# Weight decoding given to VectorE from the third retention chunk on instead of the second

## The chip, the cores and the metric

The program runs on one core of one Trainium2 chip. The metric is device time in microseconds (us). TensorE (PE in the profile) does the matmuls, VectorE (DVE) and ScalarE (ACT) the elementwise work, GpSimd (POOL) a share of it, and SyncE (SP) starts nearly all DMA transfers. Each engine works through its own queue in order, and waits where an operand is not there yet.

## The reference

Three layers follow each other on 2 sequences of 768 positions, width 512, in float32.

```python
# 1. retention, 8 heads of 64, block after block (written here as the state's recurrence)
intra = (qb @ kb.T * Dmask) @ vb
inter = (qb * lam_pow) @ kv_state
kv_state = lam_block * kv_state + (kb * rev_pow).T @ vb
# 2. feed-forward layer
xn = (x - mean) / sqrt(var + 1e-6) * g_ln
x = x + relu(xn @ w_ch1) @ w_ch2          # 512 -> 2048 -> 512
# 3. four attention experts, the two best per position, weighted by a softmax over their gates
out += w_e * (softmax(causal(x @ wq_e @ (x @ wk_e).T / 8)) @ (x @ wv_e)) @ wo_e
```

The weights w_ch1 and w_ch2 come in as 64-bit floats. The kernel turns each into two float32 halves, a high and a low one, and takes three products (high by high, low by high, high by low) for each product of the reference.

## The kernel before, in words

**Retention.** The positions are cut into 12 chunks of 128 (two sequences of six), with n from 0 to 11 in the loop `while n < len(order) ...`. Pass n loads chunk n+3 (`ret_load`: a tile qk with q and k, a tile kvn with k and v, half a megabyte each), computes the scores of chunk n+1 (`ret_scores`, L326, into the PSUM tile sc), then for chunk n the product with the state (`ret_outer`, L371), the new state (`ret_state`, L361) and the inner product (`ret_inner`, L378, both products into po). `ret_decay(n+1)` lets ScalarE (L343) and GpSimd (L344) weigh k into kd, and VectorE (L347) multiply sc by the decay into a. `ret_qd` is one GpSimd multiplication (L334); `ret_sum` puts the state into st on VectorE (L388 or L390), `ret_copy` moves po to xT with three ScalarE copies (L402, L404).

The PSUM tiles sc and po share one tag of two buffers. They are taken in turn, so sc of chunk n+1 lands in the buffer that sc of chunk n had: TensorE cannot start the scores of a chunk before VectorE has finished a of the chunk before. Three buffers each serve qk and kvn, so a load waits until the chunk three places earlier has been read.

**Layer norm.** A block is 384 positions, three chunks, and there are four. Behind its third chunk a block goes through `ln_a` to `ln_d`: the mean (`mu`, L414, `mean`, L426), x minus mean on VectorE (L434), the high half of xn on ScalarE (L436), the low one on VectorE (L440), squares on ScalarE (L442), the variance. `ln_e` multiplies xT of a block by its standard deviation (columns made by TensorE, L457, the product on VectorE, L479).

**Feed-forward layer.** Hidden features are cut into 16 tiles of 128, in four groups of four. `g1` makes one hidden tile of one block by 12 matmuls (L494, h; four k-steps for each of the three products: high weights first, then low weights, then high weights with the low half of xn), ScalarE and VectorE bring it into two halves (L513, L514). `g2` and, for the first block of the first group, `g2f` (L547, yf) multiply by the second weights.

**Weight decoding.** `prep_parts(ft, i)` decodes one weight tile: ft is its feature tile, i is 0 for the first weights and 1 for the second. It has six parts with a cost each: size (0.0; ScalarE takes the absolute value, L214), clamp (0.9; VectorE, L218 and L219), top (0.7; VectorE L223, and ScalarE's high half, L229), rest (1.2; VectorE L233 and L234, and the next weight load is started on SP), less (0.7; L238) and plus (0.7; L241, the low half). The tile is written w(ft, i) below.

**Who comes when.** From `by_hand` on the order on SP, VectorE, ScalarE and GpSimd is the order of the program's text. At the end of each pass n the loop calls `room(us)`, which takes parts from the list `norm_parts`, or where that is empty from `weight_parts`, until their costs use up us: 1.5, or 3.0 where the pass also makes a hidden tile (from n = 5). The list `weight_parts` begins with the four tiles w(0,0) to w(3,0); after the last chunk come w(0,1) to w(3,1) with `ln_e(0)` ahead of the last one. In the passes behind the last chunk, `next_step` takes the first hidden tile in the written order FIRST whose weight tile and block are decoded, so a tile that is ready later lets other work go first.

Of the kernel before, what the change touches and what calls it, by code (L numbers as in the profile page):

```python
# [67 lines left out]
def model(ctx, tc, qkT, kv, lam, g_ln, w12, wat, out):  # L68
# [41 lines left out]
    def ret_load(b, c, part=None):  # L110
        if part != 1:
            qk = r2.tile([P, 2, HP, P], F32, tag="qk", name=f"qk{b}{c}", bufs=3)
            nc.sync.dma_start(qk, qkT[b, c])
            R[b, c] = dict(qk=qk)
        if part != 0:
            kvn = r2.tile([P, 2, H, D], F32, tag="kvn", name=f"kvn{b}{c}", bufs=3)
            nc.sync.dma_start(kvn, kv[b, c])
            R[b, c]["kvn"] = kvn
# [53 lines left out]
    n, free_at = PLAN_FROM, 0  # L172
# [19 lines left out]
    def load_next(k=1):  # L192
        for _ in range(k):
            if to_load:
                to_load.pop(0)()
# [125 lines left out]
    def ret_scores(n):  # L321
        r = R[order[n]]
        sc = r["sc"] = ps_big(f"sc{n}")
        for hp, h2 in HEADS:
            for kh in range(2):
                nc.tensor.matmul(sc[half(kh), h2, cols(hp)], r["qk"][half(h2), 1, hp, half(kh)],  # L326
                                 r["qk"][half(h2), 0, hp, :], start=True, stop=True, skip_group_check=True)

    def ret_qd(n):
        b, c = order[n]  # L330
        if c > 0:
            r = R[b, c]
            r["qd"] = r2.tile([P, HP, P], F32, tag="qd", name=f"qd{n}")
            nc.gpsimd.tensor_tensor(r["qd"], r["qk"][:, 0], qpow, ALU.mult)  # L334

    def ret_decay(n):
        b, c = order[n]
        r = R[b, c]
        if c < NC - 1:
            kvn = r["kvn"]  # L340
            kd = r["kd"] = r2.tile([P, H, D], F32, tag="kd", name=f"kd{n}")
            for h in range(3):
                nc.scalar.mul(kd[:, h, :], kvn[:, 0, h, :], dec[:, h, P - 1:P])  # L343
            nc.gpsimd.tensor_tensor(kd[:, 3:, :], kvn[:, 0, 3:, :],  # L344
                                    dec[:, 3:, P - 1:P].to_broadcast([P, H - 3, D]), ALU.mult)
        a = r["a"] = r2.tile([P, 2, HP, P], F32, tag="a", name=f"a{n}")
        nc.vector.tensor_mul(a, r["sc"].rearrange("p h (k i) -> p h k i", k=HP),  # L347
                             dec.rearrange("p (h k) i -> p h k i", h=2))
# [5 lines left out]
    def ret_state(n):  # L354

        b, c = order[n]
        r = R[b, c]
        if c < NC - 1:
            ps = r["ps"] = ps_mid(f"ps{n}")
            for hp, h2 in HEADS:  # L360
                nc.tensor.matmul(ps[half(h2), cols(hp, D)], r["kd"][:, h2 * HP + hp, :],  # L361
                                 r["kvn"][:, 1, h2 * HP + hp, :], start=True, stop=True, skip_group_check=True)

    def ret_outer(n):
        b, c = order[n]
        r = R[b, c]
        r["po"] = ps_big(f"po{n}")
        if c > 0:
            st = ST.pop(n - 1)
            for hp, h2 in HEADS:  # L370
                nc.tensor.matmul(out_at(r["po"], hp, h2), st[half(h2), hp, :], r["qd"][half(h2), hp, :],  # L371
                                 start=(hp < 2), stop=False, skip_group_check=True)

    def ret_inner(n):
        b, c = order[n]
        r = R[b, c]
        for hp, h2 in HEADS:
            nc.tensor.matmul(out_at(r["po"], hp, h2), r["kvn"][:, 1, h2 * HP + hp, :], r["a"][:, h2, hp, :],  # L378
                             start=(c == 0), stop=True, skip_group_check=True)

    def ret_sum(n):
        b, c = order[n]
        if c == NC - 1:
            return
        st = ST[n] = r2.tile([P, HP, D], F32, tag="st", name=f"st{n}")
        pv = R[b, c]["ps"][:, :HP * D].rearrange("p (h e) -> p h e", h=HP)
        if c == 0:
            nc.vector.tensor_copy(st, pv)  # L388
        else:
            nc.vector.tensor_tensor(st, pv, ST["old"], ALU.add)  # L390
        if c < NC - 2:

            ST["old"] = r2.tile([P, HP, D], F32, tag="old", name=f"old{n}", bufs=1)
            nc.gpsimd.tensor_tensor(ST["old"], st, qpow[:, :, P - 1:P].to_broadcast([P, HP, D]), ALU.mult)

    def ret_copy(n):
        b, c = order[n]
        r = R.pop((b, c))
        t0 = b * S + c * P
        po = r["po"][:, :, :2 * P].rearrange("p a (k i) -> p a k i", k=2)  # L400
        x = xT[:, :, t0:t0 + P].rearrange("p (k a) i -> p a k i", a=2)
        nc.scalar.copy(x[:, 0], po[:, 0])  # L402
        for h2 in range(2):
            nc.scalar.copy(x[half(h2), 1], po[half(1 - h2), 1])  # L404
# [194 lines left out]
    def room(us):  # L599
        while us > 0 and (norm_parts or weight_parts):  # L600
            cost, f = (norm_parts or weight_parts).pop(0)
            f()
            us -= cost
# [7 lines left out]
    def next_step(inside):  # L611

        for k in range(max(1, len(FIRST) - len(steps) + len(todo))):
            if ready(k, inside):
                return step(k)[2]
        return None
# [5 lines left out]
    norm_at, n = [0] * NBLK, 0  # L622
    while n < len(order) or min(norm_at) < 4 or norm_parts or weight_parts:
        if n < len(order):
            if n + 3 < len(order):
                ret_load(*order[n + 3])
                if n < 2:
                    load_next()
            if n + 1 < len(order):
                ret_scores(n + 1)  # L630
            ret_outer(n)
            ret_state(n)
            ret_inner(n)
            if n + 1 < len(order):
                ret_decay(n + 1)
            if n + 1 < len(order):
                ret_qd(n + 1)
            ret_sum(n)
            ret_copy(n)

        for blk in range(NBLK):
            if n >= NTB * (blk + 1) and norm_at[blk] < 4 and not (norm_at[blk] == 2 and blk not in XN) \
                    and not (norm_at[blk] == 1 and blk > 0 and norm_at[blk - 1] < 3):
                norm_parts += (ln_a, ln_b, ln_c, ln_d)[norm_at[blk]](blk) or []
                norm_at[blk] += 1
        if n < len(order):
            leave = next_step(True) if n >= MLP_FROM else None
            if n > 0:
                room(ROOM[leave is not None])
            if leave:  # L650
                leave()
        if n == len(order) - 1:
            rp.close()
            ap_ = ctx.enter_context(tc.tile_pool(name="ap", bufs=HX, side="right", reuse_waits="tile"))
            WPOOL2[0] = mp.enter_context(tc.tile_pool(name="wpool2", bufs=1, side="right", reuse_waits="tile"))
            weight_parts += later_parts
        if n >= len(order):
            for _ in range(2):
                leave = next_step(False)
                room(ROOM_MLP)  # L660
                if leave:
                    leave()
        n += 1
# [308 lines left out]
```

## Time and profile before

| | us |
|---|---|
| median of 3 runs | 476.39 (474.23 to 476.47) |
| the profiled execution | 477.41 |
| its span, first to last instruction | 475.6 |
| TensorE busy in the span | 462.1 (97%) |
| VectorE busy | 340.0 (71%) |
| ScalarE busy | 202.9 (43%) |
| GpSimd busy | 86.0 (18%) |

The 1.8 us between the profiled time and its span lie around the program. The span falls into a retention stage (to about 63 us), a feed-forward stage (to about 336 us) and an attention stage. In the first, chunk after chunk goes through all five engines and the loads; afterwards TensorE has work almost without a break.

### The profile page before, as it was taken

To read this page: it belongs to the slowest core of one execution; us is meant where nothing else is said; L and a number is where in the kernel's file an instruction comes from. 1 tells how busy PE (TensorE), PEld (TensorE's weight loads), DVE (VectorE), ACT (ScalarE), POOL (GpSimd) and SP (SyncE) were. 2 spreads that over 40 slices of the span, in tenths; PEclk is the share of its full clock that TensorE was granted. 3 is DMA by queue.
4 is the path that set the end of the run, shared out by engine and by line. 5 is a ranking of instruction groups with operands and counts; after the bars stand their busy time and mean duration, and the time that the engine had idled before them with its cause. 6 is when DMAs were issued, how large, how long until landed. Compare 5 with 4: busy or idle time off the path is not lost.

```text
span 475.6 us, 9173 instructions
## 1 busy us (share of the span) xinstructions
PE 462.1 (97%) x3630; PEld 430.8 (91%) x3630; DVE 340.0 (71%) x707; ACT 202.9 (43%) x471; POOL 86.0 (18%) x132
## 2 busy tenths in 40 slices
PE   6799999999999999999999999999999999999996
PEld 4676779999999999999999999999998898998885
DVE  4688888979999787626789725435679686586663
ACT  2558675412334222202234312212356666647672
POOL 6556400000000000000000000000055444344340
PEclk8999999999999999999999999999999999999999
DMA  7986211222232231201233200000000000000011
GB/s 283 370 308 234 97 45 45 90 88 74 90 109 92 91 124 46 89 1 44 65 113 96 83 1 0 2 1 1 1 0 1 24 22 24 23 1 33 36 46 66
DMA packets 10842, 35.20 MB, mean 74 GB/s; under 512 B 1456, under 2 KB 1712, under 8 KB 10800
## 3 DMA queue, kind: packets, MB, share of 16 engines
q1 hardware_dynamic: 10512, 34.49, 21.1%
q8 instruction: 28, 0.46, 0.4%
q10 hardware_dynamic: 288, 0.13, 0.1%
q14 instruction: 14, 0.11, 0.1%
HBM read 31.47 MB, written 3.15 MB: 73 GB/s over the span
## 4 chain that ended last, share of the span: by engine, by line
PE 84%; DVE 9%; ACT 4%; DMA 1%; issue 1%; POOL 0%; SPq 0%; ACTq 0%; DVEq 0%
PE h L494 27%; PE y L528 26%; PE pj L730 4%; PE s L810 4%; PE av L859 4%; PE o L880 4%; PE t L847 4%; PE pv L752 3%; PE yf L547 2%; DVE a L347 2%; DMA qk<-in_qkT 1%; PE sc L326 1%; DVE xn L440 1%; PE po L378 1%; DVE qs L738 1%
## 5 line engine op out<-in xcount | busy, mean ns | idle before, releaser
L494 PE MATMUL h<-xn,w 128*128 128x384 f32 x768 | 140.0, 336 | 0.0
L494 PEld LDWEIGHTS h<-xn,w 128*128 128x128 f32 x768 | 133.3, 188 | 3.1 <-PE va L414 0.6
L528 PE MATMUL y<-hs,w 128*128 128x384 f32 x552 | 99.8, 334 | 0.0
L528 PEld LDWEIGHTS y<-hs,w 128*128 128x128 f32 x552 | 96.1, 188 | 0.0
L513 ACT ACTIVATE hs<-h 128x384 fp32r<-128x384 f32 x50 | 24.5, 490 | 103.0 <-PE h L494 89.4
L744 POOL TENSOR_SCALAR kh<-kh 64x384 fp32r<-64x384 f32 x16 | 8.4, 524 | 299.8 <-DVE qs L738 288.2
L514 DVE SCALAR_TENSOR_TENSOR hs<-h,hs 128x384 fp32r<-128x384 f32 x50 | 27.7, 555 | 41.4 <-ACT hs L513 41.4
L533 DVE TENSOR_TENSOR xT<-xT,y 128x768 f32<-128x768 f32 x30 | 28.5, 951 | 31.6 <-PE y L528 31.6
L837 POOL TENSOR_SCALAR att<-att,c,gw 128x128 f32<-128x128 f32 (+5 forms) x48 | 35.8, 750 | 51.7 <-DVE c L834 16.3
L229 ACT CAST w<-top 128x512 fp32r<-128x512 f32 x32 | 19.9, 620 | 52.9 <-DVE top L223 50.9
L730 PE MATMUL pj<-x,wa 128*128 128x384 f32 x192 | 35.0, 337 | 0.0
L730 PEld LDWEIGHTS pj<-x,wa 128*128 128x128 f32 x192 | 33.4, 188 | 0.0
L848 ACT COPY aT<-t 128x512 f32<-128x512 f32 (+3 forms) x64 | 26.5, 442 | 11.1 <-PE t L847 10.8
L847 PE MATMUL t<-ident,att 128*128 128x128 f32 x168 | 26.2, 275 | 0.5 <-DVE qs L738 0.5
L214 ACT ACTIVATE mag<-raw 128x512 f32<-128x512 f32 x32 | 21.1, 666 | 7.1 <-DVE w L241 7.1
L859 PE MATMUL av<-aT,v 128*64 128x128 f32 x336 | 23.6, 280 | 0.0
L810 PE MATMUL s<-kh,qs 128*128 128x512 f32 (+3 forms) x64 | 23.3, 366 | 0.0
L234 DVE SCALAR_TENSOR_TENSOR mag<-raw,mag 128x512 f32<-128x512 uint32 x32 | 22.8, 711 | 0.6
L238 DVE TENSOR_TENSOR top<-top,w 128x512 f32<-128x512 f32 x32 | 22.4, 700 | 0.0
L223 DVE SCALAR_TENSOR_TENSOR top<-raw,mag 128x512 int32<-128x512 int32 x32 | 22.0, 687 | 0.5
L241 DVE TENSOR_TENSOR w<-top,mag 128x512 fp32r<-128x512 f32 x32 | 22.0, 686 | 0.4
L859 PEld LDWEIGHTS av<-aT,v 128*64 128x64 f32 x336 | 17.8, 136 | 4.4 <-issue 3.9
(127 smaller groups left out, 720.4 us busy)
## 6 DMA issues: line engine op xcount, KB each, us to landing
raw<-in_w SPq DMA_DIRECT2D x32, 512.0 KB, 3.7
qk<-in_qkT SPq DMA_DIRECT2D x12, 512.0 KB, 6.2
kvn<-in_kv SPq DMA_DIRECT2D x12, 512.0 KB, 5.2
out<-os SPq DMA_DIRECT2D x11, 256.0 KB, 2.0
rawa<-in_wat SPq DMA_DIRECT2D x3, 512.0 KB, 3.2
rawa<-in_wat SPq DMA_DIRECT2D x1, 520.0 KB, 3.7
out<-os SPq DMA_DIRECT2D x1, 128.0 KB, 1.7
out<-os ACTq DMA_DIRECT2D x1, 128.0 KB, 1.7
```

Source lines behind the costliest of these rows:

```text
L234: nc.vector.scalar_tensor_tensor(mag, RAW[ft, i][:, :, 0].bitcast(U32), 2.0 ** -52, mag, ALU.mult, ALU.mult)
L494: nc.tensor.matmul(ph[:, :TB], w[:, wi, k, :], xn[:, xi, k, :], start=(i == 0), stop=(i == 11))
L513: LAST.append((nc.scalar.activation(h[:, 0], ph[:, :TB], AF.Relu), nc.vector.scalar_tensor_tensor(h[:, 1], ph[:, :TB], 0.0, h[:, 0].bitcas ...
L514: nc.vector.scalar_tensor_tensor(h[:, 1], ph[:, :TB], 0.0, h[:, 0].bitcast(F32), ALU.max, ALU.subtract)))
L528: nc.tensor.matmul(y[:, j, :TB], w[:, wi, e * P:(e + 1) * P], h[:, xi], start=(f == 0 and i == 0), stop=(f == GF - 1 and i == 2))
L533: nc.vector.tensor_tensor(xv, xv, y[:, :, :TB], ALU.add)
L730: nc.tensor.matmul(ps[:, :TB], w[:, wi, k, :], x2[:, xi, k, :], start=(i == 0), stop=(i == 11))
L810: nc.tensor.matmul(ps[:, c0:c1], q, kk[:, e, c0:c1], start=(i == 0), stop=(i == 1))
L837: nc.gpsimd.tensor_scalar(a[:, :n], a[:, :n], c, gw, ALU.mult, ALU.mult)
L847: nc.tensor.transpose(pt[:, (j - j0) * P:(j - j0 + 1) * P], a[:, j * P:(j + 1) * P], ident)
L848: nc.scalar.copy(aT[:, j0 * P:j1 * P], pt[:, :(j1 - j0) * P])
L859: nc.tensor.matmul(pav[e2 * HD:(e2 + 1) * HD, pr * P:(pr + 1) * P], v[:, j, e * HD:(e + 1) * HD], row["aT"][e][:, j * P:(j + 1) * P], star ...
```

## The change

One number in the loop over the chunks: `room` is first called at the end of pass n = 2 instead of n = 1. Nothing is added or removed; the weight parts are handed out one pass later, and each further `room` call takes other parts than before.

```diff
--- before.py
+++ after.py
@@ -645,7 +645,7 @@
                 norm_at[blk] += 1
         if n < len(order):
             leave = next_step(True) if n >= MLP_FROM else None
-            if n > 0:
+            if n > 1:
                 room(ROOM[leave is not None])
             if leave:
                 leave()
```

Names in the rows below: a3 is a of chunk 3, mag0_0 and top0_0 are temporaries of w(0,0), h2_1 is hidden tile 2 of block 1; the number after the last underscore only numbers the tile. First VectorE's queue behind the state of chunk 1, before the change:

```order
L390 TENSOR_TENSOR st1_308<-ps1_282,old0_245 128x256
L218 TENSOR_SCALAR mag0_0_315<-mag0_0_315 128x512
L219 TENSOR_SCALAR mag0_0_315<-mag0_0_315 128x512
L223 SCALAR_TENSOR_TENSOR top0_0_316<-raw0_0_138,mag0_0_315 128x512
L347 TENSOR_TENSOR a3_375<-sc3_327,dec_105 128x1024
L390 TENSOR_TENSOR st2_379<-ps2_353,old1_310 128x256
L233 TENSOR_SCALAR mag0_0_315<-top0_0_316 128x512
L234 SCALAR_TENSOR_TENSOR mag0_0_315<-raw0_0_138,mag0_0_315 128x512
L238 TENSOR_TENSOR top0_0_316<-top0_0_316,w0_0_321 128x512
L347 TENSOR_TENSOR a4_443<-sc4_395,dec_105 128x1024
```

The same place after the change:

```order
L390 TENSOR_TENSOR st1_308<-ps1_282,old0_245 128x256
L347 TENSOR_TENSOR a3_367<-sc3_319,dec_105 128x1024
L390 TENSOR_TENSOR st2_371<-ps2_345,old1_310 128x256
L218 TENSOR_SCALAR mag0_0_378<-mag0_0_378 128x512
L219 TENSOR_SCALAR mag0_0_378<-mag0_0_378 128x512
L223 SCALAR_TENSOR_TENSOR top0_0_379<-raw0_0_138,mag0_0_378 128x512
L347 TENSOR_TENSOR a4_438<-sc4_390,dec_105 128x1024
L390 TENSOR_TENSOR st3_442<-ps3_416,old2_373 128x256
L233 TENSOR_SCALAR mag0_0_378<-top0_0_379 128x512
L234 SCALAR_TENSOR_TENSOR mag0_0_378<-raw0_0_138,mag0_0_378 128x512
L238 TENSOR_TENSOR top0_0_379<-top0_0_379,w0_0_384 128x512
L347 TENSOR_TENSOR a5_508<-sc5_465,dec_105 128x1024
```

The first three decode instructions have gone from before a3 to before a4, the next three from before a4 to before a5. On ScalarE L214 and L229 of this tile go with them, on SP the load of the fourth weight tile falls behind the loads of chunk 6.

The second place is VectorE's queue where the last of the first weights, w(3,0), is finished, about the mean of block 3. Before:

```order
L238 TENSOR_TENSOR top3_0_1061<-top3_0_1061,w3_0_1104 128x512
L241 TENSOR_TENSOR w3_0_1104<-top3_0_1061,mag3_0_1060 128x512
L218 TENSOR_SCALAR mag0_1_1128<-mag0_1_1128 128x512
L219 TENSOR_SCALAR mag0_1_1128<-mag0_1_1128 128x512
L514 SCALAR_TENSOR_TENSOR hs2_1_1125<-h2_1_1112,hs2_1_1125 128x384
L470 RECIPROCAL rs2_1141<-std2_1139 128x3
L434 TENSOR_TENSOR dq3_1145<-xT_155,mean3_1143 128x768 x2
L514 SCALAR_TENSOR_TENSOR hw0_2_1160<-h0_2_1147,hw0_2_1160 128x384
L440 SCALAR_TENSOR_TENSOR xn3_1146<-dq3_1145,g_sb_114,xn3_1146 128x384 x4
L514 SCALAR_TENSOR_TENSOR hw1_2_1182<-h1_2_1169,hw1_2_1182 128x384
L223 SCALAR_TENSOR_TENSOR top0_1_1129<-raw0_1_654,mag0_1_1128 128x512
```

After:

```order
L470 RECIPROCAL rs2_1134<-std2_1132 128x3
L434 TENSOR_TENSOR dq3_1138<-xT_155,mean3_1136 128x768 x2
L514 SCALAR_TENSOR_TENSOR hs2_1_1153<-h2_1_1140,hs2_1_1153 128x384
L440 SCALAR_TENSOR_TENSOR xn3_1139<-dq3_1138,g_sb_114,xn3_1139 128x384 x4
L514 SCALAR_TENSOR_TENSOR hw1_2_1175<-h1_2_1162,hw1_2_1175 128x384
L238 TENSOR_TENSOR top3_0_1099<-top3_0_1099,w3_0_1120 128x512
L241 TENSOR_TENSOR w3_0_1120<-top3_0_1099,mag3_0_1098 128x512
L218 TENSOR_SCALAR mag0_1_1200<-mag0_1_1200 128x512
L219 TENSOR_SCALAR mag0_1_1200<-mag0_1_1200 128x512
```

The two instructions that finish w(3,0), and the two that begin w(0,1), have moved behind the layer norm of block 3. TensorE has the hidden tile h0_2 ahead of that mean now instead of behind it, and h2_1 behind it instead of ahead; in both orders three hidden tiles stand between the mean and h3_0, the first that reads w(3,0).

The third place is VectorE's queue at w(3,1), the last of the second weights. Before:

```order
L479 TENSOR_TENSOR xT_155<-xT_155,sb0_1333 128x2x384 x2
L514 SCALAR_TENSOR_TENSOR hx2_1279<-h0_3_1318,hx2_1279 128x384
L218 TENSOR_SCALAR mag3_1_1353<-mag3_1_1353 128x512
L219 TENSOR_SCALAR mag3_1_1353<-mag3_1_1353 128x512
L223 SCALAR_TENSOR_TENSOR top3_1_1354<-raw3_1_1210,mag3_1_1353 128x512
L233 TENSOR_SCALAR mag3_1_1353<-top3_1_1354 128x512
L234 SCALAR_TENSOR_TENSOR mag3_1_1353<-raw3_1_1210,mag3_1_1353 128x512
L238 TENSOR_TENSOR top3_1_1354<-top3_1_1354,w3_1_1359 128x512
L514 SCALAR_TENSOR_TENSOR hs1_3_1374<-h1_3_1361,hs1_3_1374 128x384
L241 TENSOR_TENSOR w3_1_1359<-top3_1_1354,mag3_1_1353 128x512
```

After:

```order
L479 TENSOR_TENSOR xT_155<-xT_155,sb0_1347 128x2x384 x2
L218 TENSOR_SCALAR mag3_1_1367<-mag3_1_1367 128x512
L219 TENSOR_SCALAR mag3_1_1367<-mag3_1_1367 128x512
L223 SCALAR_TENSOR_TENSOR top3_1_1368<-raw3_1_1226,mag3_1_1367 128x512
L514 SCALAR_TENSOR_TENSOR hs1_3_1366<-h1_3_1353,hs1_3_1366 128x384
L233 TENSOR_SCALAR mag3_1_1367<-top3_1_1368 128x512
L234 SCALAR_TENSOR_TENSOR mag3_1_1367<-raw3_1_1226,mag3_1_1367 128x512
L238 TENSOR_TENSOR top3_1_1368<-top3_1_1368,w3_1_1373 128x512
L241 TENSOR_TENSOR w3_1_1373<-top3_1_1368,mag3_1_1367 128x512
```

The half of a hidden tile, hs1_3, now stands between the tile's third and fourth decode instruction. TensorE's columns sb0, which the L479 read, have moved behind the second yf step. Before, TensorE had sb0, then yf of feature tile 1, h1_3, yf of tile 2, h2_3 and yf of tile 3; now yf of tile 1, then sb0, h1_3, yf of tile 2, h2_3 and yf of tile 3. Behind this place all engines have the same order as before.

## Rows read from the trace of the kernel before

**Rows 1.** Page, part 1: busy us, share of the span, instructions
```profile
PE 462.1 (97%) x3630; PEld 430.8 (91%) x3630; DVE 340.0 (71%) x707; ACT 202.9 (43%) x471; POOL 86.0 (18%) x132
```
**Rows 2.** Chain that ended last, at the fourth chunk: start us, us, what
```profile
20.59 1.23 DVE a L347
```
**Rows 3.** Timeline of TensorE, retention: start us, us, instruction [idle before <-releaser]
```profile
18.61 1.05 PE L378 MATMUL po<-a,kvn 128*64 128x128 f32 x16
21.86 1.98 PE L326 MATMUL sc<-qk 64*64 64x128 f32 x32 [2.21 <-DVE a L347]
...
26.34 0.85 PE L414 MATMUL mu<-xT,sum_w 128*32 128x384 f32 x8
27.12 1.10 PE L326 MATMUL sc<-qk 64*64 64x128 f32 x32
...
30.92 1.10 PE L326 MATMUL sc<-qk 64*64 64x128 f32 x32
...
38.79 1.10 PE L326 MATMUL sc<-qk 64*64 64x128 f32 x32 [0.98 <-DVE a L347]
```
**Rows 4.** Timeline of VectorE, the first decoded tiles
```profile
18.56 1.39 DVE L219 TENSOR_SCALAR mag<-mag 128x512 int32<-128x512 int32 x1
...
24.56 1.21 DVE L347 TENSOR_TENSOR a<-sc,dec 128x1024 f32<-128x1024 f32 x1
...
29.17 0.43 DVE L219 TENSOR_SCALAR mag<-mag 128x512 int32<-128x512 int32 x1
```
**Rows 5.** Timeline of ScalarE, same stretch
```profile
16.35 0.74 ACT L404 COPY xT<-po 64x256 f32<-64x256 f32 x2
17.12 0.66 ACT L214 ACTIVATE mag<-raw 128x512 f32<-128x512 f32 x1
```
**Rows 6.** Timeline of GpSimd, same stretch
```profile
18.20 1.46 POOL L334 TENSOR_TENSOR qd<-qk,qpow 128x512 f32<-128x512 f32 x1
```
**Rows 7.** Timeline of SP: issue of qk of chunks 4 and 5
```profile
13.55 0.38 SPq L113 DMA_DIRECT2D qk<-in_qkT  x1
...
16.89 0.45 SPq L113 DMA_DIRECT2D qk<-in_qkT  x1
```
**Rows 8.** DMA issues, these two: KB, us from issue to landing
```profile
qk<-in_qkT SPq DMA_DIRECT2D x1, 512.0 KB, 6.3
...
qk<-in_qkT SPq DMA_DIRECT2D x1, 512.0 KB, 8.0
```
**Rows 9.** Windows: length; busy us (instructions) by engine; PE clock, DMA share, GB/s
```profile
21.70:25.10 3.40, 3.24 (x56) 2.91 (x58) 3.37 (x6) 2.17 (x8) 2.88 (x3) 0.50 0.73 259
...
38.80:45.00 6.20, 6.20 (x100) 4.97 (x101) 5.67 (x8) 4.32 (x12) 5.38 (x6) 1.00 0.53 165
```
**Rows 10.** Timeline of TensorE, from the mean of block 3 on
```profile
74.45 0.89 PE L426 MATMUL mean<-mus,part_w 128*128 128x384 f32 x2
74.88 8.79 PE L494 MATMUL h<-xn,w 128*128 128x384 f32 x48
...
93.51 0.83 PE L457 MATMUL sb<-ident,std 128*128 128x128 f32 x6
...
102.53 2.24 PE L547 MATMUL yf<-hs,w 128*128 128x384 f32 x12
```
**Rows 11.** Timeline of VectorE, same stretch
```profile
75.65 1.79 DVE L434 TENSOR_TENSOR dq<-xT,mean 128x768 f32<-128x768 f32 x2
...
82.21 0.68 DVE L223 SCALAR_TENSOR_TENSOR top<-raw,mag 128x512 int32<-128x512 int32 x1
...
95.16 1.81 DVE L479 TENSOR_TENSOR xT<-xT,sb 128x768 f32<-128x768 f32 x2
...
101.14 0.68 DVE L241 TENSOR_TENSOR w<-top,mag 128x512 fp32r<-128x512 f32 x1
```
**Rows 12.** Timeline of ScalarE, at w(3,1)
```profile
98.99 0.62 ACT L229 CAST w<-top 128x512 fp32r<-128x512 f32 x1 [4.23 <-DVE top L223]
99.52 0.48 ACT L513 ACTIVATE hs<-h 128x384 fp32r<-128x384 f32 x1
```

## The prediction, made before the changed kernel ran

> **What bounds the kernel now.** I read the page's busy times first: TensorE works in 97% of the span [rows 1], so only the places where it stands still can be won or lost, and new ones count in full. The chain that ended last comes second. In the retention stage it does not stay on TensorE: at the fourth chunk it runs through VectorE's a [rows 2], which stood behind the first three decode instructions of w(0,0). The timelines show what that did. TensorE finished chunk 2 at 18.61 + 1.05 = 19.66 and began the scores of chunk 4 only at 21.86, after 2.21 us idle [rows 3]. It then ran at the lower of its two clocks: the granted share is 0.50 from 21.7 to 25.1, that is 1.2 instead of 2.4 GHz [rows 9]. So the decode in pass 1 costs a wait and a slow stretch. From the mean of block 3 on, TensorE's timeline has no gap for a long time (one row of 48 matmuls, four hidden tiles in 8.79 us) [rows 10]; there a later weight tile would turn into a wait that does not exist now.
>
> **Part 1, what goes: the wait before the scores of chunk 4.** After the change a of chunk 3 no longer waits for the decode and is done long before 19.66. What is late next is a load. The qk of chunk 4 is issued at 13.55 and lands 6.3 later, at 19.85 [rows 7, 8]; nothing ahead of it on SP changes. So the scores begin at about 19.9 instead of 21.86: 2.0 us earlier, and with only 0.25 us idle.
>
> **Part 2, where it goes: the scores of chunk 5.** Pass 2 now has the decode. ScalarE can take the absolute value only after its three copies of chunk 2, which follow TensorE's 19.66 with 3 x 0.37 = 1.1 us (two took 0.74), so from 20.85 to 21.5 [rows 5]. The three VectorE instructions lasted from the end of that value, 17.12 + 0.66 = 17.78, to the start of a at 20.59: 2.8 us [rows 2, 5]. That is long because GpSimd worked on qd at the same time: L219 took 1.39 beside it and 0.43 at 29.17 without it [rows 4, 6]. The bounds for the new place are 2.8 and about 1.6 (2.8 less the 0.96 of L219 and some 0.3 for the instruction before it). I take 2.8: the kvn of chunk 4 arrives at about 21.2 by the order of the loads, between the two qk landings, so GpSimd's kd and qd start just as the decode does.
>
> The Trainium skill, SBUF — State Buffer, section "Who interferes with whom", says that VectorE in its two-port mode and GpSimd exclude each other for a whole instruction, and whoever starts first keeps the port. The trace agrees (1.39 against 0.43). By that rule the decode is stretched again; without it the scores of chunk 5 would start at the landing of their qk instead, 0.6 us earlier than below.
>
> So a of chunk 4 starts at 21.5 + 2.8 = 24.3 and ends 1.2 later, at 25.5. The qk of chunk 5 lands at 16.89 + 8.0 = 24.9 [rows 7, 8], so with a short decode the load would be the bound. The scores of chunk 5 begin at 25.5 instead of 27.12 [rows 3]: 1.6 us of gain (2.2 at the other bound). TensorE in the meantime does chunk 3 and the mu matmuls, which it did from 26.34 to 27.12 before [rows 3], and is through with them at about 23.75; it idles 1.75 us.
>
> **Part 3, the scores of chunk 6.** The next three decode instructions and st sat between two a's 24.56 - 20.59 = 4.0 us apart [rows 2, 4]. The same now lies between a of chunk 4 and a of chunk 5: 24.3 + 4.0 = 28.3, ending at 29.5. TensorE is ready about then, since 27.12 to 30.92 are 3.8 us [rows 3], and 25.5 + 3.8 = 29.3. So the scores of chunk 6 start at 29.55 instead of 30.92, which is **-1.35 us**. This assumes that the clock does not fall in the 1.75 us gap. It did after 2.21 us [rows 3, 9]; it did not after 0.98 us at 38.79, where the share stays at 1.00 [rows 3, 9]. 1.75 lies between. If it falls, the gain is given back: in the slow stretch the work from 21.86 to 26.34 took 4.5 us where the same work after 27.12, without the 0.84 or so of the mean, took 3.0, so 1.5 more and nothing is left. The range of this term is -2.2 to 0; I take -1.35, since nothing in the trace shows a fall after less than 2.2 us idle in the middle of steady chunks. From there to the mean of block 3 the chunks carry the shift along; the pieces of decode between them are the same ones in another order, and I cost them at nothing. The load of the fourth weight tile slips behind those of chunk 6, has some 40 us until it is used, and gives their loads its place: also nothing. Neither SP nor GpSimd gets other work.
>
> **Part 4, a new wait at w(3,0).** Now count from the mean's start, 74.45 [rows 10], as zero. VectorE needs the mean itself (0.89), so it starts x minus mean at +0.94 at the earliest. From there before, 75.65, to the decode instruction that followed the layer norm, 82.21, there were 6.56 us [rows 11], in which it waits for ScalarE's high half of xn and for a hidden tile. After the change L238 and L241 stand at that place, 0.72 and 0.69: w(3,0) is complete at 0.94 + 6.56 + 1.41 = +8.9. TensorE has three hidden tiles after the mean. Four took 8.79 from 74.88 on; less some 0.4 for the change of kind of matmul they are 2.08 each. So h3_0 begins at 0.43 + 0.4 + 6.25 = +7.1, and its fifth matmul, the first with low weights, at +7.75. It waits **1.2 us**. Before, the two instructions were done ahead of the mean, so there was no wait.
>
> **Part 5, a new wait at w(3,1).** Before, w(3,1) was ready at 101.14 + 0.68 = 101.82, and yf of tile 3 began at 102.53 [rows 10, 11]: 0.7 us to spare. Now count from TensorE's sb0 (93.51 before) as zero; sb0 has moved one yf step nearer to its end. The L479 starts when sb0 is done, +0.88. From L479 to the end of L241 there were 101.82 - 95.16 = 6.66 us [rows 11]. One hidden half (0.47) stands no longer in between, but the other one does so ahead of L233, and waits until ScalarE, which gets top at that moment, has done its cast and its own half: 98.99 to 100.00, 1.0 us [rows 12] and some 0.1 of hand-over. That is 6.66 - 0.47 + 1.1 = 7.3, so w(3,1) is ready at +8.2. TensorE wants it after 0.59 of sb0, 2.19 for h1_3, and 2.08 each for yf of tile 2 and h2_3, and with the second matmul already: 6.94 + 0.17 = +7.1. It waits **1.1 us**. For VectorE to be free for L479 at +0.88, its work from w(3,0) on has to fit; it comes to some 14.3 us against TensorE's 14.3, so it just does.
>
> Bounds of the two waits together: four decode instructions more behind the mean are 0.72 + 0.69 + 0.45 + 0.45 = 2.3 us for VectorE, less the 0.9 to spare at w(3,1), so 1.4 if VectorE never idles; and 3.4 if it comes to L479 late by as much as the second wait again. I take 2.3, the sum by the rows. Behind it all engines have the old order and TensorE no gap, so nothing of it is won back.
>
> **Sum.** -1.35 + 1.2 + 1.1 = +0.95 us against the profiled execution (span 475.6, time 477.41 with 1.8 around it). That execution lies 1.0 above the median of 476.39; I put the difference on the median: **477.3 us**. The bounds give -2.2 + 1.4 = -0.8 to 0 + 3.4 = +3.4, that is 475.6 to 479.8.
>
> **The rivals.** Differences under 0.5%, 2.4 us, cannot be told from none in a measurement of this kernel (its three runs are 2.2 apart).
>
> *The clock falls in the new gap.* TensorE starts chunk 5 at half clock after 1.75 us idle, part 3 is worth nothing, and the waits stay: +2.3, 478.7. For it speaks that the decode is moved, not shortened; against it that mu fills a part of the gap. Half of this case lies above the 2.4.
>
> *The waits cost the clock too (slower).* The two new waits on low weights, 1.2 and 1.1, are longer than the 0.98 after which the clock stayed up. If it falls at each, the restart costs about the 1.5 us of the slow stretch twice: 0.95 + 3.0, 480.3. It decides from the length of idle at which the clock goes. Against it: around these waits TensorE is busy throughout.
>
> *The decode keeps up.* The decode in pass 2 is short, the load bounds (-2.2), and VectorE fills its idle so that only 1.4 of waits is left: -0.8, 475.6.
>
> *The waits do not come at all.* TensorE takes longer over its hidden tiles than I count, w(3,0) and w(3,1) are in time, and the early gain stays: -1.35 to -2.7 (the gain of part 2 with further shorter waits), 474.2 or so. Against it stand the fixed orders at both places.
>
> *Nothing is moved.* Excluded: VectorE's queue is another one.
>
> **How the numbers follow.** My forecast has 0.50, the fallen clock 0.22, the waits with the clock 0.10, the decode that keeps up 0.12, no waits 0.06. Slower by over 0.5%, above 478.8: all of 0.10, half of 0.22, and 0.03 of the forecast's edge, 0.24. Faster: 0.06, where the gain without waits meets a low run. Within: 0.70. The range reaches from 475.0, which takes in the kept-up decode with a little for the spread of runs, to 479.8, the upper bound of the sum.
>
> **What would show it.** Part 1: the scores of chunk 4 start near 19.9, released by their load. Part 2: those of chunk 5 near 25.5, released by VectorE's a, and L219 again over 0.8 us. Part 3: the granted clock is 1.00 from 21 to 29, and chunk 6 starts near 29.5. Part 4: in the first h3 TensorE stops about 1.2 us, released by L241. Part 5: the same in the fourth yf step, about 1.1. I am wrong if TensorE has no gaps between the mean of block 3 and the fourth yf step, or if that mean does not come earlier than 74.45.

## The result, and the profile after

| us | before | changed |
|---|---|---|
| median (range, runs) | 476.02 (474.23 to 477.19, 10) | 479.47 (477.09 to 481.33, 10) |
| the profiled execution, its span | 477.41, 475.6 | 480.25, 477.4 |
| mean of block 3, start | 74.45 [rows 10] | 73.52 |
| from there to the end of the span | 401.15 | 403.88 |

The ratio is 1.0062, with a 95% interval of 1.0043 to 1.0080: slower by about 3 us (the two medians lie 3.45 apart). The range of 475.0 to 479.8 holds the time, but the centre, 477.3, is 2 us low, and the side it fell on had a chance of 0.24.

The busy times, the page's first part, are nearly those of [rows 1]: the same work, otherwise spaced.

```profile
span 477.4 us, 9174 instructions
PE 462.1 (97%) x3630; PEld 429.7 (90%) x3630; DVE 340.4 (71%) x707; ACT 202.6 (42%) x471; POOL 84.5 (18%) x132
```

In the timeline of TensorE the retention stage answers to [rows 3]: start, length, instruction, idle before it and its releaser.

```profile
20.20 1.10 PE L326 MATMUL sc<-qk 64*64 64x128 f32 x32 [0.57 <-DMA qk<-in_qkT]
...
23.16 1.34 PE L414 MATMUL mu<-xT,sum_w 128*32 128x384 f32 x8
25.83 1.10 PE L326 MATMUL sc<-qk 64*64 64x128 f32 x32 [1.32 <-DVE a L347]
...
30.34 1.10 PE L326 MATMUL sc<-qk 64*64 64x128 f32 x32 [0.20 <-DVE a L347]
```

Chunk 4 now waits for its load and starts at 20.20 (21.86 before). Chunk 5 waits for VectorE's a, 25.83 (27.12), chunk 6 starts at 30.34 (30.92). The clock did not fall in the new gap; of the window that had 0.50 in [rows 9]:

```profile
21.70:25.10 3.40, 2.81 (x43) 1.58 (x40) 3.33 (x4) 0.43 (x1) 1.93 (x2) 1.00 1.03 371
```

An earlier stretch at the lower clock, ahead of all that the change moves, is in both profiles, and the prediction does not mention it: the granted clock from 6 to 12 us averages 0.72, and within it is 0.50 from 9 to 11. Before, then after:

```profile
6.00:12.00 6.00, 4.53 (x92) 3.96 (x94) 3.75 (x6) 1.65 (x6) 5.52 (x15) 0.72 1.03 418
...
6.00:12.00 6.00, 4.53 (x90) 3.96 (x92) 3.73 (x6) 1.65 (x6) 5.52 (x15) 0.72 1.02 416
```

VectorE's timeline, as [rows 4], shows what stands ahead of the two a's at 24.56 and 29.07, and GpSimd's, as [rows 6], what runs beside it.

```profile
21.55 0.95 DVE L218 TENSOR_SCALAR mag<-mag 128x512 f32<-128x512 f32 x1 [2.26 <-ACT mag L214]
22.54 1.38 DVE L219 TENSOR_SCALAR mag<-mag 128x512 int32<-128x512 int32 x1
...
24.56 1.22 DVE L347 TENSOR_TENSOR a<-sc,dec 128x1024 f32<-128x1024 f32 x1
...
27.39 1.76 DVE L238 TENSOR_TENSOR top<-top,w 128x512 f32<-128x512 f32 x1
29.07 1.21 DVE L347 TENSOR_TENSOR a<-sc,dec 128x1024 f32<-128x1024 f32 x1
```

```profile
22.18 1.45 POOL L334 TENSOR_TENSOR qd<-qk,qpow 128x512 f32<-128x512 f32 x1
...
26.88 1.72 POOL L334 TENSOR_TENSOR qd<-qk,qpow 128x512 f32<-128x512 f32 x1
```

Both times the stretched instruction, L219 (1.38) and L238 (1.76), lies beside GpSimd's qd. L238 takes 0.68 at 81.05, where GpSimd has no work. In the kernel before it was stretched too, but less, and beside kd:

```profile
23.42 1.22 DVE L238 TENSOR_TENSOR top<-top,w 128x512 f32<-128x512 f32 x1
...
22.91 1.18 POOL L344 TENSOR_TENSOR kd<-kvn,dec 128x320 f32<-128x320 f32 x1
```

From the mean of block 3 on TensorE's timeline, without a gap in [rows 10], has two stops:

```profile
73.52 0.89 PE L426 MATMUL mean<-mus,part_w 128*128 128x384 f32 x2
73.96 7.40 PE L494 MATMUL h<-xn,w 128*128 128x384 f32 x40
82.51 1.66 PE L494 MATMUL h<-xn,w 128*128 128x384 f32 x8 [1.16 <-DVE w L241]
...
96.10 0.83 PE L457 MATMUL sb<-ident,std 128*128 128x128 f32 x6
...
103.04 0.34 PE L547 MATMUL yf<-hs,w 128*128 128x384 f32 x1
104.39 2.20 PE L547 MATMUL yf<-hs,w 128*128 128x384 f32 x11 [1.02 <-DVE w L241]
```

The 40 matmuls are three hidden tiles and the four of h3_0 with high weights; then TensorE waits for the low half of w(3,0). In the fourth yf step it stops after one matmul, for the low half of w(3,1). VectorE's timeline has the two L241 that end these waits, and what delays the second:

```profile
74.45 1.82 DVE L434 TENSOR_TENSOR dq<-xT,mean 128x768 f32<-128x768 f32 x2
...
81.76 0.69 DVE L241 TENSOR_TENSOR w<-top,mag 128x512 fp32r<-128x512 f32 x1
...
96.97 1.82 DVE L479 TENSOR_TENSOR xT<-xT,sb 128x768 f32<-128x768 f32 x2 [0.18 <-PE sb L457]
...
101.39 0.56 DVE L514 SCALAR_TENSOR_TENSOR hs<-h,hs 128x384 fp32r<-128x384 f32 x1 [1.08 <-ACT hs L513]
...
103.65 0.69 DVE L241 TENSOR_TENSOR w<-top,mag 128x512 fp32r<-128x512 f32 x1
```

Up to the mean of block 3 the changed kernel is 0.93 us ahead of the execution shown before, and behind it 2.73 later. In the span that makes +1.8.

### The profile page after: what moved, and what is told of

Same layout as the page of the kernel before. It is cut to its first block, busy times and chain, and to the rows that moved or that the text cites. A ratio compares the mean times of both kernels' runs of the same rounds, so it can differ in the third digit from the quotient of the medians.

```text
span 477.4 us, 9174 instructions
## 1 busy us (share of the span) xinstructions
PE 462.1 (97%) x3630; PEld 429.7 (90%) x3630; DVE 340.4 (71%) x707; ACT 202.6 (42%) x471; POOL 84.5 (18%) x132
## 4 chain that ended last, share of the span: by engine, by line
PE 79%; DVE 11%; ACT 4%; DMA 3%; issue 1%; POOL 1%; SPq 0%; DVEq 0%; ACTq 0%; POOLq 0%
PE y L528 26%; PE h L494 24%; PE pj L730 4%; PE s L810 4%; PE av L859 4%; PE o L880 4%; PE t L847 4%; PE pv L752 3%; DMA qk<-in_qkT 3%; DVE a L347 2%; PE yf L547 1%; DVE xn L440 1%; ACT xn L436 1%; PE sc L326 1%; DVE top L238 1%
## 5 line engine op out<-in xcount | busy, mean ns | idle before, releaser
L229 ACT CAST w<-top 128x512 fp32r<-128x512 f32 x32 | 19.8, 619 | 52.9 <-DVE top L223 52.9
L214 ACT ACTIVATE mag<-raw 128x512 f32<-128x512 f32 x32 | 21.3, 671 | 7.1 <-DVE w L241 7.1
L238 DVE TENSOR_TENSOR top<-top,w 128x512 f32<-128x512 f32 x32 | 24.0, 749 | 0.0
L241 DVE TENSOR_TENSOR w<-top,mag 128x512 fp32r<-128x512 f32 x32 | 22.0, 686 | 0.5
```

What stands on the lines that cost most here:

```text
L238: nc.vector.tensor_tensor(t["top"], t["top"], t["w"][:, 0].bitcast(F32), ALU.subtract)
```

## The experiments

The theory: the loss is the two waits of parts 4 and 5, and the gain ahead of them is smaller than forecast. The rivals: the decode in retention costs the loss itself; the second wait is only the first passed on; the clock decides. Of every run two numbers are worth most: the ratio to the kernel before, and in its profile the time from the mean of block 3 to the end of the span, which holds the waits but nothing of the retention stage. "Mean span" is over the timed runs; for the kernel before it is 474.97 (the 98 runs beside the experiments, those of e1 among them). The last two columns are of the one profiled execution of each.

| run | ratio [95%] | mean span | mean of block 3 | from there to the end |
|---|---|---|---|---|
| e1 same | 1.0002 [0.9988, 1.0016] | 475.05 | 72.91 | 401.1 |
| e2 tail repaid | 1.0011 [1.0000, 1.0022] | 475.59 | 74.24 | 401.2 |
| e3 tail late | 1.0064 [1.0038, 1.0089] | 476.97 | 72.22 | 403.9 |
| e4 size early | 0.9984 [0.9970, 0.9998] | 474.03 | 72.66 | 401.0 |
| e5 first wait | 1.0037 [1.0017, 1.0057] | 476.79 | 74.36 | 402.4 |
| e6 second wait | 1.0037 [1.0024, 1.0049] | 476.96 | 73.55 | 402.4 |
| e7 gap filled | 0.9995 [0.9981, 1.0008] | 474.55 | 73.36 | 401.3 |
| e8 size one pass early | 1.0002 [0.9990, 1.0013] | 474.92 | 74.56 | 401.1 |
| e9 repaid in pass 6 | 1.0050 [1.0031, 1.0069] | 477.53 | 76.97 | 401.1 |
| e10 size early, repaid | 1.0030 [1.0016, 1.0045] | 476.38 | 74.26 | 401.0 |
| e11 changed again | 1.0057 [1.0035, 1.0079] | 477.57 | 72.62 | 403.8 |
| e12 size early, load late | 0.9994 [0.9979, 1.0010] | 474.86 | 74.44 | 401.0 |

**e1, the kernel before, unaltered.**

> The kernel before, unchanged, run as if it were a new one. If the change really costs 3.4 us in the median while the two profiled spans differ by only 1.8, either the profiled execution of before was a slow one of its kind, or time outside the span has grown. Mine: this run's spans lie mostly near 474 to 475, below the 475.6 that was profiled, because in most executions the clock does not fall after the 2.21 us gap; where a profile shows no fall between 15 and 30 us, the mean of block 3 starts near 73 instead of 74.45. Rival: spans stay at 475.6 and the difference is outside the span. The ratio to before should be 1.000 within 0.003 for both.

It shows that the kernel before has two kinds of execution. Here the scores of chunk 4 waited even longer than in [rows 3], and the clock stayed up:

```profile
21.18 1.10 PE L326 MATMUL sc<-qk 64*64 64x128 f32 x32 [2.34 <-DVE a L347]
...
72.91 0.89 PE L426 MATMUL mean<-mus,part_w 128*128 128x384 f32 x2
```

```profile
21.00:25.00 4.00, 3.62 (x88) 2.79 (x88) 3.96 (x6) 2.49 (x9) 3.46 (x3) 1.00 0.92 343
```

Its mean of block 3 comes at 72.91, not 74.45. Not all of the 1.54 us arises at chunk 4. The early stretch is missing in e1 as well, and in e11, the second set of runs of the changed kernel; e1, then e11:

```profile
6.00:12.00 6.00, 5.41 (x112) 4.67 (x116) 3.87 (x6) 1.94 (x7) 5.54 (x16) 1.00 1.02 416
...
6.00:12.00 6.00, 5.41 (x103) 4.61 (x107) 3.85 (x6) 1.70 (x7) 5.53 (x15) 1.00 1.02 416
```

So the scores of chunk 4 start 0.68 earlier in e1 (21.18, 21.86), and the other 0.86 comes behind them. Over 98 runs of this kernel, 40 have a mean granted clock of 0.999 or 1.0 and spans of 474.2 on average, 58 one of 0.996 or less and 475.5; it was expected that most would not fall. The execution that the prediction argued from is of the second kind: it has both stretches and a mean clock of 0.993, and 42 of the 58 lie at 0.992 or 0.993. For a run that was not profiled the mean does not say where its clock was low. For the changed kernel (16 runs) the spans do not follow the clock so: 477.2 for the eight with 0.999 or more, 477.4 for the other eight.

**e2, the changed kernel, with the parts it holds back made up for in pass 11, and e3, the kernel before, with as much held back in pass 11.**

```diff
-                room(ROOM[leave is not None])
+                room(ROOM[leave is not None] + (1.6 if n == 11 else 0.0))
```

This is e2; e3 has - 1.6 in its place, and `n > 0` as before.

> The change, and in pass 11 room is given 1.6 us more, so that from the last chunk on every engine has the order of before; the retention passes 2 to 10 stay as changed. My theory (the loss is the two waits for w(3,0) and w(3,1), the retention part is a small gain of 0.9 in the profiles): no TensorE gap at the first h3 nor at the fourth yf step, mean of block 3 near 73.5 to 74.5 (pass 11 now carries 1.6 us more on VectorE), time 2 to 3 us under the changed kernel, that is within 1 us of before. Rival (the loss is made in the retention passes, by the decode falling on GpSimd's work and on the loads): stays 2 us or more above before.

> The kernel before, and in pass 11 room is given 1.6 us less, so that retention up to pass 10 is as before and from then on the order is that of the changed kernel. My theory: both waits are there, 1.2 and 1.1 us, and the early gain is not: 2.3 to 3 us slower than before. Rival (the loss is made in retention): no slower than before by more than 0.5 us.

e3 has the whole loss with nothing changed in retention until pass 11, and both stops:

```profile
81.20 1.68 PE L494 MATMUL h<-xn,w 128*128 128x384 f32 x8 [1.15 <-DVE w L241]
...
103.10 2.20 PE L547 MATMUL yf<-hs,w 128*128 128x384 f32 x11 [1.01 <-DVE w L241]
```

e2 has neither, and 401.2 behind the mean. That settles where the loss is. But e2 is no faster than the kernel before, and has a small stop of its own for w(2,0), which gets late in its order. From the scores of chunk 11 to the mean of block 3 it takes 18.94 us (55.30 to 74.24), the kernel before 18.28 (56.17 to 74.45):

```profile
70.08 3.74 PE L494 MATMUL h<-xn,w 128*128 128x384 f32 x20 [0.51 <-DVE w L241]
```

**e5 and e6, one wait each.** e5 makes up for the parts in pass 14; e6 makes up in pass 11 and holds back again in pass 14.

```diff
-                room(ROOM_MLP)
+                room(ROOM_MLP + (1.6 if n == 14 and _ == 0 else 0.0))
```

This is e5, on the changed kernel; e6 has e2's line and - 1.6 here.

> The changed kernel up to w(3,0), whose last two instructions stay behind the layer norm of block 3; two passes later the parts held back are made up for (one room call in pass 14 gets 1.6 us more), so that every queue from the third tile of the second weights on is that of the kernel before. Theory (the two waits are separate and each costs what its shift in the trace of the changed kernel shows, 1.43 for w(3,0) and 1.44 for w(3,1)): one stop of about 1.1 us in the first h3, released by VectorE's L241, none in the fourth yf step; from there about 1.4 later than the run with the tail repaid (477.39), so 478.8 us, ratio to the kernel before about 1.004. Rival A (the second wait is only the first one's delay passed on along VectorE, so it comes in any case): two stops, ratio 1.006. Rival B (VectorE wins the first wait back before the end): ratio 1.001.

> The reverse: the tail repaid at n = 11, so that w(3,0) is done ahead of the mean of block 3, and one room call of pass 14 gets 1.6 us less, so that from there on every queue is that of the changed kernel. Theory (separate waits): no stop in the first h3, one of about 1.0 us in the fourth yf step, released by L241; 477.4 + 1.4 = 478.8 us, ratio about 1.004. Rival A (the second wait is the first one's delay passed on): no stop at all, ratio 1.001. Rival B (TensorE, which now comes to the fourth yf step 1.4 us earlier than in the changed kernel while VectorE is bound by its own work, waits longer there): one stop of over 2 us, ratio 1.006.

Each has its own stop alone. First e5, then e6:

```profile
83.34 1.68 PE L494 MATMUL h<-xn,w 128*128 128x384 f32 x8 [1.15 <-DVE w L241]
```

```profile
102.99 2.20 PE L547 MATMUL yf<-hs,w 128*128 128x384 f32 x11 [1.02 <-DVE w L241]
```

Behind the mean of block 3 they take 402.4 each, 1.3 more than 401.1; with both it is 403.9, 2.7 more. The waits add, and the second is not the first passed on.

**e7, the kernel before with two matmuls in the gap ahead of the scores of chunk 4.** Their result is read by nobody.

```diff
+                if n == 3:
+                    fp = ps_mid("fillps")
+                    for _ in range(2):
+                        nc.tensor.matmul(fp[:, :TB], part_w, dec[:, 0:3, :], start=True, stop=True)
                 ret_scores(n + 1)
```

> The kernel before with two more matmuls (the form of the mean, 128x384, on constants, into a PSUM tile that nothing reads) on TensorE's queue ahead of the scores of chunk 4, where it idles 2.2 us; nothing else is different. Theory (the idle there lets the clock fall in about two executions of three, 1.3 us each; spans of the kernel before average 474.2 without and 475.5 with a fall): the idle shrinks to about 0.4 us, the scores of chunk 4 start where they did (21.2 to 21.9), the granted clock is 1.00 from 20 to 40, and the spans average 474.2 instead of 475.0: ratio 0.9983, about 476.0 us. Rival A (the fall comes from something other than this gap, or is not what separates the executions): spans as before, ratio 1.000. Rival B (the two matmuls delay the scores): ratio above 1.000, some 1 us more at the most.

```profile
19.55 1.56 PE L633 MATMUL fillps<-dec,part_w 128*128 128x384 f32 x4
21.62 1.10 PE L326 MATMUL sc<-qk 64*64 64x128 f32 x32 [0.51 <-DVE a L347]
```

```profile
21.00:25.00 4.00, 3.29 (x81) 2.64 (x80) 3.97 (x6) 2.62 (x10) 3.03 (x3) 1.00 0.78 282
```

The idle shrank to 0.51, the clock stayed up there, and the group of spans near 475.5 thinned out: the five runs with a mean clock of 0.996 or less average 474.8 (17 of the kernel before beside them 475.5), the six others 474.4 (474.2). The profiled execution has the early stretch (0.996 in the mean) and only that; of the 17 runs before, 16 had 0.992 or 0.993, of these five two. That fits the theory that the idle is what lets the clock fall at chunk 4. The ratio alone does not tell it from no change: only half of the runs before had a fall this time, and the extra matmuls seem to cost 0.2.

**e4 and e8, the absolute value of the first tile handed out earlier**: in pass 0 of the kernel before (e4), and in pass 1 of the changed kernel with the tail repaid in pass 11 (e8).

```diff
+            if n == 0:
+                weight_parts.pop(0)[1]()
             if n > 0:
```

This is e4; in e8 it is `n == 1`, with `n > 1` below and e2's line.

> The kernel before, and only the first part of the first weight tile, ScalarE's absolute value, is given out at the end of pass 0 instead of pass 1. VectorE's order is untouched. Before, VectorE stood idle 2.24 us before the decode, waiting for that value. My theory: decode runs from about 15.6 to 17.3, the scores of chunk 4 are released by their load at 19.9 instead of 21.86, the clock does not fall, no new wait comes later: 1.5 to 2.5 us faster than before. Rival (the loads bound the retention passes, or GpSimd's work stretches the decode there too): within 0.5 us of before.

> The changed kernel with the tail repaid, and with ScalarE's absolute value of the first weight tile handed out in pass 1, one pass ahead of its clamp; nothing else differs from the run with the tail repaid. Theory (in the changed kernel the decode in pass 2 is late because VectorE waits 2.26 us for that absolute value, L218 at 21.55): L218 starts at about 19.5 to 20, a of chunk 4 is no longer behind the decode, and the load bounds the scores of chunk 5, which start at 25.2 instead of 25.83 and those of chunk 6 at 29.2 to 29.4 instead of 30.34; the mean of block 3 comes 0.9 us earlier than with the tail repaid; ratio to the kernel before 0.999, about 476.2 us. Rival A (the stretch of VectorE's instructions beside GpSimd, not the wait for the value, sets the scores): chunk 5 at 25.8, ratio 1.001. Rival B (the load bounds chunk 5, but the decode in pass 3 keeps chunk 6 at 30.3): ratio 1.001.

e4 is the only version whose interval lies below 1. In it the decode no longer holds up a, the scores of chunk 4 start at 20.35 without idle, and the spans average 474.03 in both halves by clock: it gains what the fall costs (0.9 by the mean spans; 1.5 to 2.5 were expected). In e8 the early part went as the theory said, VectorE's L218 at 19.61 instead of 21.55 and L219 less stretched:

```profile
19.61 0.42 DVE L218 TENSOR_SCALAR mag<-mag 128x512 f32<-128x512 f32 x1
20.06 0.72 DVE L219 TENSOR_SCALAR mag<-mag 128x512 int32<-128x512 int32 x1
```

```profile
25.25 1.10 PE L326 MATMUL sc<-qk 64*64 64x128 f32 x32
...
29.05 1.10 PE L326 MATMUL sc<-qk 64*64 64x128 f32 x32
```

But the mean of block 3 came at 74.56, later than in e2: the 1.3 us in hand at chunk 6 were gone by chunks 7 to 9, at two stops told of in the last section and again at w(2,0), 0.50.

**e9, the held-back parts made up for in pass 6 instead of 11, and e10, e9 with e8's early value.**

```diff
+                room(ROOM[leave is not None] + (1.6 if n == 6 else 0.0))
```

> The changed kernel with 1.6 us more for room in pass 6: from the second tile's top on every queue is that of the kernel before, TensorE's whole order too, so that only the decode of w(0,0) and of the half of w(1,0) is late. With the tail repaid in pass 11, w(2,0) was late too: the first h2 stopped 0.51 us for it (70.08, released by L241) and the mean of block 3 came 0.7 later than it could. Theory (that stop took away what the early part had won): no stop on a weight tile anywhere; from the mean of block 3 to the end 401.1 us as before; mean of block 3 near 73.5; spans average 474.9 against 475.6 with the tail repaid in pass 11, about 476.7 us, ratio to the kernel before 0.999 to 1.000. Rival A (the early part as such is worth its forecast of -1.35 once nothing else is late): ratio 0.997. Rival B (the stop was covered by other idle time, so nothing changes): 1.001.

> The same, and ScalarE's absolute value of the first tile handed out in pass 1. Its run with the tail repaid in pass 11 had the scores of chunks 5 and 6 at 25.25 and 29.05 but the stop of 0.50 at w(2,0), and spans that average 474.9. Theory: no stop, so 0.7 less, spans near 474.2, 476.1 us, ratio 0.9985, the same as with the absolute value early in the order of the kernel before (0.9984). Rival (the loads of chunks 7 and 8, which landed late in that profile, take the gain whatever VectorE does): ratio 1.000.

Both expectations were wrong. No weight tile is late any more, and behind the mean the time is 401.1; but pass 6 now puts six decode instructions, where the kernel before has three, ahead of a of chunk 8, and VectorE waits for ScalarE's value in their midst (e9):

```profile
41.45 0.43 DVE L218 TENSOR_SCALAR mag<-mag 128x512 f32<-128x512 f32 x1 [2.44 <-ACT mag L214]
...
44.17 1.22 DVE L347 TENSOR_TENSOR a<-sc,dec 128x1024 f32<-128x1024 f32 x1
```

It is like the wait of chunk 4 in the kernel before, later in the stage, but TensorE does not feel it at once: the scores of chunk 9 come 6.68 after those of chunk 8 (39.87 to 46.55), as in the kernel before (38.79 to 45.48). One chunk later VectorE's delay reaches it. TensorE stood still ahead of the scores of chunk 10 and its clock fell, to 0.72 on average from 50 to 55:

```profile
51.64 1.46 PE L326 MATMUL sc<-qk 64*64 64x128 f32 x32 [1.30 <-DVE a L347]
```

```profile
50.00:55.00 5.00, 3.70 (x71) 3.29 (x72) 3.72 (x6) 4.56 (x12) 2.54 (x3) 0.72 0.66 256
```

This profile is of the slowest of the six runs and lost time ahead of pass 6 too: the clock was low from 10 to 14 us, and again from 35 to 38 behind a wait of 1.91 for the load of chunk 7. So how much of e9's loss belongs to pass 6 is not shown.

**e11, the changed kernel once more, and e12, e4 with the fourth weight load behind the loads of chunk 6.**

```diff
-            load_next()
+            if (ft, i) != (0, 0):
+                load_next()
...
-                if n < 2:
+                if n < 2 or n == 3:
```

> The changed kernel once more, unaltered, beside the others. If the time outside the span (2.4 us on average in its first 10 runs, 1.8 to 1.9 in the kernel before and in the two kernels with one of the two waits) belongs to this kernel, it is 2.3 to 2.5 again and the ratio 1.006; if it belonged to that set of runs, it is near 1.9 and the ratio 1.0045 to 1.005. From the mean of block 3 to the end: 403.9 us again under both.

> The kernel before with the absolute value of the first tile handed out in pass 0 (0.9984 when it ran alone), and the load of the fourth weight tile started behind the loads of chunk 6 instead of ahead of them, as the change has it. Theory (from 10 to 30 us the DMA engines are busy over 95%, so each load ahead of a chunk's delays it): the loads of chunk 6 land some 1.2 us earlier, the scores of chunks 6 to 8 come up to 1 us earlier, ratio 0.996 to 0.9975. Rival (the chunks are bound by their own chain through VectorE and GpSimd there, so the load's place is worth nothing): 0.9984 again.

e11 has both stops again (1.15 and 1.01) and 403.8 behind the mean; its time outside the span averages 2.17, between the two expectations (1.76 to 2.08 in five runs, 3.53 in one). e12 fell on the rival's side or worse: the scores of chunks 5 and 6 came early, at 24.63 and 28.43, and the mean of block 3 at 74.44 all the same, behind a stop of 2.30 (last section) and a granted clock of 0.50 from 32 to 35.

## Why the prediction was right or wrong

**Part 1, right.** Scores of chunk 4 at 20.20, released by their load; forecast 19.9.

**Part 2, right in kind for an execution like the one read.** 25.83 for 25.5, released by a, L219 stretched again. The decode took 3.0 from 21.55 to 24.56, not 2.8. In e11, without the early stretch, L219 took 0.43, and the scores of chunk 5 began at 24.52 without idle:

```profile
24.52 1.10 PE L326 MATMUL sc<-qk 64*64 64x128 f32 x32
28.58 1.10 PE L326 MATMUL sc<-qk 64*64 64x128 f32 x32 [0.18 <-DVE a L347]
32.78 1.10 PE L326 MATMUL sc<-qk 64*64 64x128 f32 x32 [1.64 <-DVE xn L440]
```

**Part 3, the term that failed: -1.35.** Three things were off. The three instructions and st were taken to fill 4.0 us between the two a's; it was 29.07 - 24.56 = 4.5, since L238 now fell beside GpSimd's qd (1.76) instead of kd (1.22). The Trainium skill, SBUF — State Buffer, section "Who interferes with whom", says that an instruction of VectorE with two inputs from this memory contends with one of GpSimd that reads it. The trace agrees (L238 1.76 there, 0.68 alone). The prediction asked what GpSimd would do beside the pieces of pass 2 and not beside those of pass 3. So chunk 6 gained 0.58.

Nor do the chunks simply carry the shift along, which was put at nothing. In the two profiles it grew to 0.93 at the mean of block 3, as the wait of 0.98 ahead of chunk 8 [rows 3] went too (37.32 instead of 38.79). Between e1 and e11, which both lack the early stretch, it shrank: 1.10 at the scores of chunk 6 (29.68, 28.58), then a wait of 1.64 ahead of chunk 7 instead of 0.63, and 0.29 at the mean (72.91, 72.62).

The larger error is the start. The profiled execution had the clock fall that the change removes and the early stretch that it does not, and the prediction put the whole difference on the median as if every execution were like it. With the time behind the mean subtracted from the mean spans, the mean of block 3 stood at 475.5 - 401.1 = 74.4 in the 58 runs before with a lower clock, 474.2 - 401.1 = 73.1 in the 40 without, 73.85 over all. In the 16 runs of the changed kernel it is 477.28 - 403.83 = 73.45. The early part is worth -0.4, and the spread of the runs leaves it uncertain by another 0.4 or so, so it can hardly be told from nothing. By single executions it is -0.93 where both have the early stretch and -0.29 where neither has.

**Parts 4 and 5, right.** x minus mean started at +0.93 (forecast +0.94), w(3,0) was complete at 82.45, +8.9 (+8.9), and TensorE waited 1.16 (1.2). L479 started +0.87 behind sb0 (+0.88), the hidden half waited 1.08 for ScalarE (1.1), w(3,1) was complete at 104.34, +8.2 (+8.2), and TensorE waited 1.02 (1.1). Only what a wait costs beyond its idle was left out: 1.3 each in e5 and e6 and 2.7 for both, where the sum had 2.3.

**The sum.** By means over all runs: -0.4 ahead of the mean, +2.7 behind it, and +0.45 outside the span (2.3 instead of 1.85), together +2.75 us. The forecast was -1.35 + 2.3 = +0.95.

**The rivals.** The clock did not fall in the gap of chunk 5, nor at the two waits (1.00 from 80 to 86 and from 102 to 106), so neither rival came, though the first, at 478.7, is nearer to the time measured than the forecast. "The decode keeps up" and "the waits do not come" are refuted by the rows of the changed kernel: in e11 the decode did keep up with chunk 5, but both waits were there in full. Missing among the rivals was the case that the profile shown was itself one of the longer executions.

## What to carry to other kernels

Work that is handed out from one list moves as a whole: what is taken from the front of a list by one pass is missing at its end, and the price is read there, at the last tile that someone waits for. Before a gain is counted in full, see whether the profiled execution is typical: a wait that sometimes drops the clock is worth what it costs on average. Where a piece waits for a producer on another engine, try bringing forward that producer alone: here that was the only gain measured (e4, 0.9984; in the changed order, e8, the ratio was 1.0002), while moving the whole lost.

## What the runs showed of the hardware

**The clock after a stop varies between executions.** After 2.21 us idle ahead of chunk 4 it fell to 0.50 (1.2 GHz), after 2.34 at the same place in e1 it stayed at 1.00 (2.4 GHz), and in e9 it fell with a stop of 1.30. In e11 it stayed up after 1.64. The length of one gap doesn't decide it here. Nor does the granted clock tell all: e1's first scores, at 5.93, took 1.98 us under a clock shown as 1.00, those of the kernel before, at 5.96, took 1.10. The Trainium skill, TensorE: Matmul & The Clock Gate, section "Part 1: The HAM clock gate (the "warmup" mystery)", says that the chip's watch on the engine runs freely and isn't reset when a kernel starts; that one program starts with 1.98 in one execution and 1.10 in another agrees with it.

**A stop that no engine explains.** In the four kernels with the early absolute value (e4, e8, e10, e12), and in e3 without it, TensorE stopped in the midst of the product of chunk 5 with its state, always after 5 of 16 matmuls, for 1.04, 1.48, 0.60, 2.30 and 0.84 us. In e12, then e3:

```profile
29.36 0.40 PE L372 MATMUL po<-qd,st 64*64 64x128 f32 x5
32.06 1.12 PE L372 MATMUL po<-qd,st 64*64 64x128 f32 x11 [2.30 <-issue]
...
30.95 0.65 PE L371 MATMUL po<-qd,st 64*64 64x128 f32 x11 [0.84 <-issue]
```

"issue" means that it waited for nothing the profile shows. There are two more such places, 125 matmuls ahead of this one (e9, 0.68) and 126 behind it (e8 and e10, 0.64 and 1.21, in the scores of chunk 8). From 29 to 32 the view of e12's transfers has one packet of instructions among 263 of data:

```profile
q1 hardware_dynamic: 263, 0.96, 93.8%
q8 instruction: 1, 0.02, 1.9%
```

A load of instructions that is late behind the data would explain the fixed places, and the 14 traces fit it: at each of the three places TensorE goes on no sooner than 2.2 us after such a packet has started, and in all eight stops 2.2 to 2.5 us after it. In e12 that is from 29.61 to 32.06, in e3 from 28.50 to 30.95, while in the kernel before the packet started at 28.66, 3.3 us ahead of the same matmul, and there is no stop. No run moves the packet alone, so the cause is not proven. It is one place where the gain of e8, e10 and e12 went.

**Time outside the span.** It is 1.85 us in the kernel before, 1.8 in e5 and e6, but 2.4 and 2.2 in the two sets of the changed kernel and 2.7 in e3, the kernels with both waits. In these it is 1.8 to 2.1 in some runs and 2.5 to 3.5 in others. Its cause stays open.
